# Another order of loads and units, and V of batch 0 sorted on TensorE, in a fused block-sorted attention and token-mixing kernel

## The chip, the cores and the metric

The kernel runs on one core of one Trainium2 chip. The metric is the time of one execution on the device in microseconds (us), the median over runs. A profile is of one execution; its times count from the first instruction.

## The reference, cut to what matters

The input has 4 batches of 8 heads, 768 rows of 64. The rows form 8 blocks of 96. K and V are mixed over blocks with an 8x8 matrix P for each head, which five rounds of row and column normalisation make out of sort_net. Attention works inside each block. Then a token mixer without softmax follows.

```
for _ in range(5):
    P = exp(P - max(P)); P = P / (sum_rows(P) + 1e-9); P = P / (sum_cols(P) + 1e-9)
k_sorted = einsum('bhij,bhjcd->bhicd', P, k_b)      # the same for v
x = softmax(scale * q_b @ k_sb.T) @ v_sb            # in each block of 96 rows
W = scale * (x @ w_q) @ (x @ w_k).T                 # 768 x 768 for each batch
out = relu(W @ x) @ w_out
```

## The kernel before, in words

**The order.** Nothing is scheduled by the compiler. A table of tokens, ORDER, is read from left to right, and each token calls one function u_*, which issues the instructions of one unit on the engines that the token names. Each engine keeps the order of its own instructions and waits for data and buffers by semaphores. A token is a kind, a batch, a number, and after colons an engine (A ScalarE, D VectorE, G GpSimd, S SyncE) or a PSUM bank, or both. A capital letter is work on TensorE into a bank, the small letter its eviction out of the bank:

- l: a load of one batch of q, k or v, or of weights (lp: w_q and w_k, lo: w_out). GpSimd issues it; it turns f32 in memory to bf16 (768 KB written). There are three buffers each for Qn, Kn and Vn, so batch 3 goes into batch 0's.
- a, c: the five normalisation rounds, on ScalarE and VectorE in turn. B spreads the result, and n makes the mixing matrices M of a batch (two buffers). Batch 0's M is made on VectorE out of PSUM, the others on GpSimd out of the copy PTR, in two instructions each.
- Z: fillers, products of zeros without use, so many as the number says.
- Q, q: turns Qn on TensorE (QT). K, k: sorts and turns Kn by a product with M (KT). In QT and KT the columns lie over the partitions.
- V, v: sorts Vn in three units, evicted to the one buffer Vs. Six SyncE DMAs (R, 132 KB each) regroup the rows of Vs into VT, in which the rows of a block lie over the partitions.
- S, e: scores and exponentials (E). P, r, x: product with VT (five units, the last a short one with 8 products in place of 14), reciprocal of the row sums, and scaling into X. One P unit needs all six R of its batch.
- T, t: turns X (XT). J, j: product with w_q and w_k (qkT). d: copies half of qkT to qD, on other partitions. W, w: turns qkT (wk). G, g: product of X and wk (Ab). H, h: product of Ab with qkT and qD, relu (mixT). O, o, s: product with w_out, eviction, output DMA.
- N: the gate. GpSimd copies one element of VT that all six R of a batch must have written; GpSimd's later loads stand behind it.

Y, y, F and f exist and are not in this order: they sort and turn V as K is sorted (into the KT buffer of the other batch), and turn it back in blocks of 96 rows into VT, without a DMA.

**Where the work waits.** GpSimd's queue holds the loads, M for batches 1 to 3 and four gates. SyncE's queue holds R, six of the eight qD copies and the output. A last part on GpSimd (guard) reads the reciprocals and decides whether a slow general path is run; it isn't. Line 147 is the matmul helper, 151 and 153 the copy helper on ScalarE and VectorE, so groups of the profile are told apart by tiles.

Of the kernel before, what the change touches and what calls it, by code (L numbers as in the profile page):

```python
# [16 lines left out]
ORDER = """
i02:D c00:D i00:G lq0 a01:A c01:D a02:A c02:D Z019:0 Q03:0 a03:A c03:D a04:A Q00:1 c04:D Q02:2 lq1
a05:A c05:D lv0 Z010:3 B00:3 lk0 n00:D:3 q00:A:1 n03:D:3 n02:D:3 Q13:1 i03:G Q11:4 q02:A:2 q03:D:0
Q12:2 q13:A:1 n01:D:3 Q01:5 Z011:6 V01:6 V00:0 q12:D:2 v00:A:0 u00:D:3 q01:D:5 V02:2 Q10:5 lk1  # L20
v02:A:2 Z09:0 K00:0 K01:2 n10:G q10:D:5 q11:A:4 K02:4 v01:A:6 K03:6 k00:A:0 lv1 k01:D:2 n11:G
k03:A:6 S00:0 k02:D:4 S01:2 S06:6 S04:4 e01:A:2 Z03:2 K10:2 e00:A:0 K13:0 e06:A:6 R01:S S02:6
k10:D:2 k13:D:0 K12:2 S05:0 e04:A:4 n21:G S03:4 R00:S R04:S e02:A:6 k12:D:2 lk2 e05:A:0 R03:S K11:6
lq2 e03:A:4 R02:S R05:S n20:G S14:2 e14:A:2 V12:0 k11:D:6 v12:D:0 V10:6 P03:4 r03:D:4 x03:D:4 V11:2
S11:0 v10:A:6 v11:A:2 P01:6 e11:A:0 P02:4 S12:2 S13:0 r01:D:6 x01:D:6 e12:A:2 r02:D:4 K22:6 k22:A:6
K20:2 e13:A:0 P04:6 x02:D:4 S15:4 e15:A:4 k20:D:2 P00:2 S10:0 r04:D:6 Q23:4 x04:D:6 R14:S r00:D:2
Q20:5 S16:6 e10:A:0 N05:G R15:S R10:S Q22:0 x00:D:2 Q21:3 q20:D:5 e16:A:6 K23:1 K21:5 T01:7 R11:S
q22:D:0 lv2 R12:S R13:S q23:A:4 k21:A:5 q21:D:3 lp k23:D:1 P12:3 t01:A:7 T02:0 r12:D:3 P11:5
x12:D:3 r11:D:5 V20:1 lq3 T03:7 t02:A:0 T00:0 V21:3 v20:A:1 x11:D:5 P13:1 t00:D:0 t03:A:7 P14:5
v21:A:3 r13:D:1 T11:7 J01:0 V22:3 x13:D:1 r14:D:5 j01:A:0 x14:D:5 P10:1 v22:A:3 r10:D:1 t11:D:7  # L30
n30:G x10:D:1 J00:0 S23:5 S20:3 T12:7 lk3 j00:A:0 e23:A:5 t12:D:7 e20:A:3 T13:0 W01:1 W00:2 n31:G
T10:5 S24:6 w01:D:1 t13:D:0 w00:D:2 S22:3 S25:0 t10:D:5 R23:S Q30:2 e24:A:6 Q31:5 Q33:6 N15:G G00:7
e22:A:3 q30:D:2 e25:A:0 Q32:2 d01:S K32:3 lv3 q31:D:5 q33:D:6 K31:5 K33:0 G01:7 q32:D:2 R20:S
k32:A:3 R24:S k31:A:5 k33:D:0 d00:S S21:2 J10:4 e21:A:2 g00:D:7 R25:S R21:S j10:D:4 S35:5 H02:0 lo
e35:A:5 R22:S H00:2 h00:A:2 J11:7 K30:4 j11:A:7 h02:D:0 k30:D:4 S32:0 W10:6 V30:2 w10:D:6 W11:7
V32:4 e32:A:0 P23:0 w11:A:7 v32:A:4 V31:6 v30:D:2 r23:D:0 v31:A:6 O04:2 x23:D:0 R31:S P20:3 S26:0
r20:D:3 R34:S S30:5 G10:7 G11:7 e26:A:0 S33:0 x20:D:3 H01:3 e30:A:5 o04:A:2 g10:D:7 P21:5 O05:2
h01:A:3 P22:3 d11:S r21:D:5 x21:D:5 T20:7 o05:A:2 e33:A:0 r22:D:3 t20:A:7 P24:5 R35:S x22:D:3
r24:D:5 O03:2 d10:S o03:A:2 O00:0 S36:3 H10:1 R32:S x24:D:5 S31:5 o00:A:0 R30:S e31:A:5 O02:7
h10:D:1 T22:0 e36:A:3 o02:A:7 t22:D:0 S34:5 s02:S H11:1 H12:3 R33:S T21:7 e34:A:5 N25:G O01:0  # L40
t21:A:7 P33:5 h11:D:1 T23:7 P30:1 h12:A:3 t23:A:7 o01:D:0 r33:D:5 P32:3 x33:D:5 s00:S r30:D:1 J20:0
O12:5 r32:D:3 s01:S P31:6 x30:D:1 j20:D:0 x32:D:3 O10:1 r31:D:6 O11:0 J21:4 j21:A:4 P34:2 x31:D:6
T32:6 o10:A:1 d21:S T31:7 r34:D:2 t31:A:7 T30:4 W20:1 N35:G x34:D:2 t30:A:4 T33:2 t32:D:6 t33:D:2
O15:3 J30:4 w20:D:1 W21:1 J31:2 j30:A:4 W30:4 j31:D:2 O14:7 W31:2 o11:A:0 w21:A:1 G20:1 o14:A:7
d30:D w30:A:4 s10:S d20:S G21:1 w31:D:2 G30:4 o15:A:3 G31:4 g20:A:1 o12:A:5 H20:6 h20:A:6 H22:2
H21:0 d31:D g30:D:4 h22:D:2 O13:4 O21:7 o13:A:4 s11:S h21:D:0 O20:6 o20:A:6 H30:2 s12:S H31:4
h31:A:4 o21:D:7 O24:7 O25:6 O22:4 h30:D:2 O23:5 O31:3 o25:A:6 o23:A:5 o24:D:7 s20:S o22:D:4 H32:0
O30:4 s22:S o31:D:3 O33:3 s21:S h32:D:0 o33:D:3 o30:A:4 O35:0 O34:1 o34:A:1 s31:S O32:3 s30:S
o35:D:0 o32:A:3 s33:S s35:S s34:S s32:S
"""  # L50


# [1 line left out]
def kernel(  # L54
# [91 lines left out]
    def mm(o, w, x, start=True, stop=True, t=False):  # L146
        nc.tensor.matmul(o, w, x, is_transpose=t, start=start, stop=stop, skip_group_check=True)  # L147

    def copy(e, o, i):
        if e == "A":  # L150
            nc.scalar.copy(o, i)  # L151
        else:
            nc.vector.tensor_copy(o, i)  # L153
# [7 lines left out]

    def u_a(b, n, e, bank):
        nc.scalar.activation(Pv, Pv, ACT.Exp)
        if n == 2:
            for j in range(NB):
                mm(PS[:, 7, 0:SP], idb, idb[:, j * SP:(j + 1) * SP], start=(j == 0), stop=(j == NB - 1))
            nc.scalar.copy(m_p, PS[:, 7, 0:SP])
        elif n == 3:
            nc.scalar.copy(Lx.rearrange("p a j s -> p (a j) s"),
                           idb[0:BH, 0:BH].unsqueeze(2).to_broadcast([BH, BH, SP]))  # L170

    def u_c(b, n, e, bank):
        if n == 0:
# [46 lines left out]
                                in_=src[b, h0:h1].rearrange("h (p r) d -> p h (r d)", p=P))  # L220

    def u_B(b, n, bank):

# [78 lines left out]
        ENG[e].dma_start(out=VT[b % 2].rearrange("(s r) i h x -> r s i (h x)", r=R6)[n],  # L302
                         in_=Vs[0][:, n].rearrange("p h e -> p (h e)"))

    def u_N(b, n, e, bank):

        nc.gpsimd.tensor_copy(gate[0:R6, :], VT[b % 2][0:R6, NB - 1, H - 1, 0:1])  # L307
# [338 lines left out]
```

## Time and profile before

| | us |
|---|---|
| median of 3 runs | 111.21 (110.87 to 113.28) |
| span of the profiled execution | 109.3 |
| TensorE busy | 94.8 (87%), of it fillers 14.4 |
| VectorE, ScalarE, GpSimd busy | 71.1, 67.6, 26.8 |

The file gives no separate time for the profiled execution; its span is 109.3 us, 1.9 below the median of the runs, and what lies around the span is counted as these 1.9 us. In the strips of the profile a digit is a tenth of busy time in a fortieth of the span. In a group or row, the tile written stands left of the arrow and the tiles read right of it; "x" counts instructions; in square brackets stands how long the engine was idle before, and what ended that.

### The profile page before, as it was taken

Reading aid. Unit: us, or ns where it says so; the run is one execution under the profiler, and the core shown is the slowest. Engines: PE = TensorE matmul, PEld = TensorE weight load, DVE = VectorE, ACT = ScalarE, POOL = GpSimd, SP = SyncE. Lnnn points to the kernel's source line nnn. Section 1 sums busy time; section 2 is a strip of 40 time slices with the busy share of each in tenths; the row PEclk is TensorE's granted clock in tenths of the full one; section 3 lists DMA queues with packets and bytes.
Section 4 is the critical chain, followed back from the end, with each engine's and each line's share of the span. In section 5 each row is a group of like instructions: output and inputs, shape, how many; then the busy total and the mean of one; then the engine's idle time right before and its main releaser. Section 6 shows DMA issues by size and latency. Waiting matters only on the chain.

```text
span 109.3 us, 3462 instructions
## 1 busy us (share of the span) xinstructions
PE 94.8 (87%) x1460; PEld 64.3 (59%) x1460; DVE 71.1 (65%) x140; ACT 67.6 (62%) x96; POOL 26.8 (24%) x46
## 2 busy tenths in 40 slices
PE   4997999986978759999959999999999993999950
PEld 2335557463767648897948687746858672443410
DVE  2676681060959984799956898778898431974720
ACT  4224314897589874698976998899706671463240
POOL 7960029069079700330000000000004700000000
PEclk9999999999599995999999999999999999999999
DMA  0899999999999999999999914670360050097872
GB/s 3 91 201 204 203 204 206 203 235 248 229 210 199 218 254 239 188 209 202 218 242 248 201 25 117 164 244 6 127 261 17 6 218 4 40 418 309 352 307 112
DMA packets 20225, 20.16 MB, mean 185 GB/s; under 512 B 2032, under 2 KB 18288, under 8 KB 20208
## 3 DMA queue, kind: packets, MB, share of 16 engines
q0 software_dynamic: 14064, 10.09, 61.1%
q1 hardware_dynamic: 6144, 9.84, 26.7%
q8 instruction: 11, 0.18, 0.6%
q14 instruction: 6, 0.05, 0.1%
HBM read 20.19 MB, written 6.29 MB: 242 GB/s over the span
## 4 chain that ended last, share of the span: by engine, by line
PE 53%; DMA 34%; POOL 5%; issue 2%; DVE 2%; ACT 1%; POOLq 0%; ACTq 0%; DVEq 0%
PE ps L147 53%; DMA Kn<-in_k_dram 15%; DMA Qn<-in_q_dram 14%; DMA qD<-qkT 4%; POOL Qn L219 2%; POOL M L240 1%; DVE QT L153 1%; DVE KT L153 1%; POOL Kn L219 1%; POOL Vn L219 1%; ACT ot L151 1%; POOL idb L191 0%; POOL idb L190 0%; POOLq L191 0%; DVE qkT L153 0%
## 5 line engine op out<-in xcount | busy, mean ns | idle before, releaser
L321 ACT ACTIVATE E<-ps 96x960 bf16<-96x960 f32 (+1 forms) x28 | 24.1, 898 | 5.2 <-PE ps L147 5.1
L147 PE MATMUL ps<-wo,mixT 128*128 128x512 bf16 x96 | 22.7, 379 | 0.0
L350 DVE TENSOR_TENSOR X<-ps,Rall 96x896 bf16<-96x896 f32 (+1 forms) x20 | 20.1, 1005 | 0.6
L151 ACT COPY ot<-ps 128x512 f32<-128x512 f32 x17 | 10.0, 588 | 8.7 <-PE ps L147 8.0
L147 PE MATMUL ps<-fil 128*128 128x512 bf16 x52 | 14.4, 433 | 0.4 <-ACT Vs L151 0.2
L153 DVE CAST KT<-ps 128x768 bf16<-128x768 f32 x10 | 9.4, 956 | 7.7 <-PE ps L147 7.5
L147 PEld LDWEIGHTS <-mixT 128*128 128x128 bf16 x96 | 8.6, 98 | 9.4 <-issue 0.6
L151 ACT CAST Vs<-ps 128x1024 bf16<-128x1024 f32 x10 | 9.9, 1019 | 4.2 <-PE ps L147 4.0
L147 PE MATMUL ps<-VT,E 96*128 96x65 bf16 x256 | 10.9, 193 | 1.0 <-DVE X L350 0.3
L147 PEld LDWEIGHTS <-E 96*128 96x128 bf16 x256 | 9.8, 97 | 2.8 <-issue 1.3
L147 PE MATMUL ps<-idb,Qn 128*64 128x128 bf16 x192 | 8.1, 244 | 3.3 <-DMA Qn<-in_q_dram 1.9
L240 POOL TENSOR_TENSOR M<-PTR,m_p 128x512 bf16<-128x512 bf16 x6 | 7.9, 1323 | 12.1 <-DVE PTR L153 8.4
L412 DVE TENSOR_SCALAR mixT<-ps 128x1024 bf16<-128x1024 f32 x7 | 8.5, 1222 | 3.0 <-PE ps L147 3.0
L147 PE MATMUL ps<-QT,KT 64*128 64x96 bf16 x256 | 10.0, 213 | 0.4 <-DVE KT L153 0.2
L153 DVE COPY QT<-ps 128x768 bf16<-128x768 bf16 x11 | 5.9, 553 | 6.7 <-PE ps L147 6.7
L307 POOL COPY gate<-VT 6x1 bf16<-6x1 bf16 x4 | 0.7, 177 | 38.3 <-DMA VT<-Vs 38.3
L147 PEld LDWEIGHTS <-fil 128*128 128x128 bf16 x52 | 5.4, 109 | 7.4 <-issue 3.4
L147 PEld LDWEIGHTS <-Qn 128*64 128x64 bf16 x192 | 6.7, 124 | 4.6 <-DMA Qn<-in_q_dram 2.7
L147 PE MATMUL ps<-M,Kn 128*64 128x128 bf16 x192 | 8.0, 238 | 1.6 <-DMA Kn<-in_k_dram 1.3
L147 PEld LDWEIGHTS <-KT 64*128 64x128 bf16 x256 | 6.9, 99 | 3.5 <-issue 1.9
L147 PEld LDWEIGHTS <-Kn 128*64 128x64 bf16 x192 | 6.7, 121 | 3.5 <-DMA Kn<-in_k_dram 2.2
L147 PE MATMUL ps<-idb,X 96*128 96x96 bf16 x128 | 7.5, 206 | 0.0
(74 smaller groups left out, 129.0 us busy)
## 6 DMA issues: line engine op xcount, KB each, us to landing
out_dram<-ot SPq DMA_DIRECT2D x9, 512.0 KB, 3.3
VT<-Vs SPq DMA_DIRECT2D x24, 132.0 KB, 6.4
Qn<-in_q_dram POOLq DMA_DIRECT2D x4, 768.0 KB, 12.8
Vn<-in_v_dram POOLq DMA_DIRECT2D x4, 768.0 KB, 14.9
Kn<-in_k_dram POOLq DMA_DIRECT2D x4, 768.0 KB, 18.1
out_dram<-ot SPq DMA_DIRECT2D x6, 256.0 KB, 2.0
wo<-in_moe_w_out_dram POOLq DMA_DIRECT2D x1, 512.0 KB, 17.4
qD<-qkT SPq DMA_DIRECT2D x6, 48.0 KB, 3.3
```

The costliest lines, as they stand in the source:

```text
L147: nc.tensor.matmul(o, w, x, is_transpose=t, start=start, stop=stop, skip_group_check=True)
L151: nc.scalar.copy(o, i)
L153: nc.vector.tensor_copy(o, i)
L219: nc.gpsimd.dma_start(out=t[b % NIN][:, h0:h1].rearrange("p h r d -> p h (r d)"), in_=src[b, h0:h1].rearrange("h (p r) d -> p h (r d)", p=P))
L240: ENG[e].tensor_tensor(out=M[b % 2][:, h0:h0 + hn], in0=src.unsqueeze(2).to_broadcast([P, hn, SP, NB]), in1=m_p.unsqueeze(1).unsqueeze(3). ...
L307: nc.gpsimd.tensor_copy(gate[0:R6, :], VT[b % 2][0:R6, NB - 1, H - 1, 0:1])
L321: nc.scalar.activation(E[b % 2][:, n, 0:2 * w * BLK].rearrange("p (t a c) -> p a t c", a=2, c=BLK), PS[0:BLK, bank:bank + 2, 0:w * BLK].re ...
L350: nc.vector.tensor_mul(xo.rearrange("p (a t d) -> p a t d", a=2, d=D), avps(bank, w)[:, :, :, 0:D], Rall[:, b, n, :, 0:w].unsqueeze(3).to_ ...
L412: nc.vector.tensor_relu(o, i)
```

## The change

The whole table ORDER is written anew. The rest of the edit is what the new table needs:

- GpSimd's queue starts with the loads of q and k of batch 0, ahead of the identity and the memsets. The loads' order was q0, q1, v0, k0, k1, v1, k2, q2, v2, w_q, w_k, q3, k3, v3, w_out; now it is q0, k0, q1, v0, v1, k1, w_q, w_k, k2, q2, w_out, v2, q3, k3, v3.
- The four gates are gone, with the buffer gate.
- V of batch 0 goes through four Y and four F units with their evictions, in place of three V and six R.
- Five of the eight qD copies run on GpSimd and three on VectorE; none is a DMA.
- Fillers are 22 in three places (52 in five before). The spreading of small constants is a unit of its own (B01, p). All other units stand in a new order, with engines and banks newly given.
- u_D, a transposing DMA, is defined and not used.

```diff
-i02:D c00:D i00:G lq0 a01:A c01:D a02:A c02:D Z019:0 Q03:0 a03:A c03:D a04:A Q00:1 c04:D Q02:2 lq1
...
+i02:D Z03:0 lq0 c00:D lk0 a01:A c01:D i00:G i03:G B01:0 p01:A a02:A p00:A:0 c02:D lq1 lv0 a03:A c03:D lv1
...
-    gate = sb.tile([P, 1], BF16, name="gate")
...
-        if n == 2:
-            for j in range(NB):
-                mm(PS[:, 7, 0:SP], idb, idb[:, j * SP:(j + 1) * SP], start=(j == 0), stop=(j == NB - 1))
-            nc.scalar.copy(m_p, PS[:, 7, 0:SP])
...
+    def u_p(b, n, e, bank):
+        if n == 0:
+            copy(e, m_p, PS[:, bank, 0:SP])
...
-    def u_N(b, n, e, bank):
-
-        nc.gpsimd.tensor_copy(gate[0:R6, :], VT[b % 2][0:R6, NB - 1, H - 1, 0:1])
...
     def u_d(b, n, e, bank):
         o, i = (t[b % 2][p:p + DH, n * 384:(n + 1) * 384] for t, p in ((qD, DH), (qkT, 0)))
-        if e == "S":
-            nc.sync.dma_start(out=o, in_=i)
+        if e == "G":
+            nc.gpsimd.tensor_copy(o, i)
         else:
             copy(e, o, i)
```

What the table does shows in the engines' queues. In the rows that follow, a name's suffix is a buffer: M_107 and M_108 are the two buffers of M (batches 0 and 2, 1 and 3), Kn_74 is batch 2's, Qn_69 and Kn_72 those of batches 0 and 3. DMASW0 to DMASW7 are the eight semaphores on which GpSimd's loads tell of their landing, taken in turn.

GpSimd before, from the second K load to the load of q of batch 3:

```order
L219 DMA Kn_73<-in_k_dram 128x8x384
L240 TENSOR_TENSOR M_108<-PTR,m_p 128x512 [waits DVE_49,Activation_49]
L219 DMA Vn_76<-in_v_dram 128x8x384
L240 TENSOR_TENSOR M_108<-PTR,m_p 128x512
L240 TENSOR_TENSOR M_107<-PTR,m_p 128x512 [waits PE_49]
L219 DMA Kn_74<-in_k_dram 128x8x384
L219 DMA Qn_71<-in_q_dram 128x8x384
L240 TENSOR_TENSOR M_107<-PTR,m_p 128x512
L307 COPY gate<-VT_85 6x1 [waits DMAHW4_49,DMAHW5_49,DMAHW3_49,DMAHW6_49,DMAHW2_49,DMAHW1_49]
L219 DMA Vn_77<-in_v_dram 128x8x384 [waits DMASW0_49]
```

GpSimd now, from the load of K of batch 2, the ninth DMA on this queue:

```order
L215 DMA Kn_74<-in_k_dram 128x8x384 [waits DMASW0_49]
L215 DMA Qn_71<-in_q_dram 128x8x384 [waits DMASW1_49]
L210 DMA wo<-in_moe_w_out_dram 128x4x512 [waits DMASW2_49]
L215 DMA Vn_77<-in_v_dram 128x8x384 [waits DMASW3_49]
L215 DMA Qn_69<-in_q_dram 128x8x384 [waits DMASW4_49,PE_49]
L239 TENSOR_TENSOR M_108<-PTR,m_p 128x512 [waits Activation_49]
L239 TENSOR_TENSOR M_108<-PTR,m_p 128x512
L215 DMA Kn_72<-in_k_dram 128x8x384 [waits DMASW5_49,PE_49]
```

M of batch 1 (M_108) stood between the first six loads; now it stands behind the load of q of batch 3, which waits for the landing of v of batch 1 (DMASW4).

ScalarE now, from the first of batch 1's three evictions of sorted V (Vs) to the last eviction ahead of the first P unit of that batch:

```order
L147 COPY Vs_84<-ps 128x8x2x64 [waits PE_49]
L147 COPY KT_83<-ps 128x768 [waits PE_49]
L147 COPY KT_83<-ps 128x768 [waits PE_49,Activation_49]
L315 ACTIVATE E_88<-ps 96x2x2x96 [waits PE_49]
L147 COPY Vs_84<-ps 128x8x2x64 [waits DVE_49,PE_49]
L147 COPY Vs_84<-ps 128x8x2x64 [waits PE_49]
L315 ACTIVATE E_88<-ps 96x2x5x96 [waits DVE_49,PE_49]
L315 ACTIVATE E_88<-ps 96x2x5x96 [waits PE_49]
L315 ACTIVATE E_88<-ps 96x2x5x96 [waits DVE_49,PE_49]
L147 COPY KT_82<-ps 128x768 [waits PE_49]
L315 ACTIVATE E_88<-ps 96x2x5x96 [waits PE_49]
L147 COPY XT_91<-ps 128x768 [waits DVE_49,PE_49]
```

Behind these come one more E and two QT evictions, then the first P unit's banks are free. Before, ScalarE had two of batch 1's three Vs evictions one behind the other:

```order
L321 ACTIVATE E_88<-ps 96x2x5x96
L151 COPY Vs_84<-ps 128x8x2x64 x2
L321 ACTIVATE E_88<-ps 96x2x5x96 x2
L151 COPY KT_82<-ps 128x768
L321 ACTIVATE E_88<-ps 96x2x5x96 x3
L321 ACTIVATE E_88<-ps 96x2x2x96
L151 COPY QT_80<-ps 128x768
```

The first of the three moved ahead of two KT evictions of the same batch; the other two stand behind them and a short E.

More of the change, by code (lines that the diff above doesn't have):

```diff
@@ L17 @@
 ORDER = """
-i02:D c00:D i00:G lq0 a01:A c01:D a02:A c02:D Z019:0 Q03:0 a03:A c03:D a04:A Q00:1 c04:D Q02:2 lq1
[L19 to L47, printed above, removed]
@@ L48 @@
-O30:4 s22:S o31:D:3 O33:3 s21:S h32:D:0 o33:D:3 o30:A:4 O35:0 O34:1 o34:A:1 s31:S O32:3 s30:S
-o35:D:0 o32:A:3 s33:S s35:S s34:S s32:S
+i02:D Z03:0 lq0 c00:D lk0 a01:A c01:D i00:G i03:G B01:0 p01:A a02:A p00:A:0 c02:D lq1 lv0 a03:A c03:D lv1
+Z010:0 lk1 a04:A c04:D lp a05:A c05:D lk2 Q03:0 lq2 Q02:1 q03:A:0 Q01:2 B00:3 lo q01:D:2 q02:A:1 Q00:0 n03:D:3
+lv2 n01:D:3 K03:1 n02:D:3 K01:4 q00:D:0 k03:A:1 lq3 K02:6 n00:D:3 k01:A:4 k02:D:6 S05:0 u00:A:3 S02:4 e05:A:0
+S03:6 n10:G S04:2 e02:A:4 Q13:0 Q11:1 n11:G q13:D:0 e03:A:6 K00:4 q11:D:1 Q10:0 k00:A:4 S06:6 lk3 Q12:1
@@ new lines @@
+e06:A:6 S00:4 q12:D:1 q10:A:0 S01:6 e01:A:6 Y03:0 y03:A:0 e04:A:2 Y01:6 Y00:0 y01:D:6 y00:A:0 n20:G F03:3
+Z09:2 f03:A:3 e00:A:4 F01:0 F00:1 f01:D:0 V12:2 f00:D:1 Y02:4 v12:A:2 P04:6 n21:G P01:0 r04:D:6 y02:A:4
+x04:D:6 P00:2 R15:S r01:D:0 R14:S lv3 K13:4 r00:D:2 x01:D:0 K11:6 k13:A:4 k11:D:6 K10:0 S16:4 x00:D:2 e16:A:4
+V11:6 V10:4 v11:A:6 k10:D:0 T00:3 n30:G F02:2 v10:A:4 t00:D:3 R13:S S11:0 f02:D:2 K12:6 R12:S e11:A:0 S10:4
+n31:G k12:D:6 R10:S P02:2 e10:A:4 P03:0 R11:S r02:D:2 x02:D:2 S13:6 K20:4 e13:A:6 r03:D:0 T01:2 x03:D:0
@@ new lines @@
+k20:A:4 S14:6 t01:D:2 e14:A:6 T03:0 K22:3 t03:A:0 K23:1 k22:D:3 S15:6 T02:5 e15:A:6 k23:D:1 Q23:4 Q20:3
+q23:A:4 Q22:6 t02:D:5 q20:D:3 q22:A:6 S12:0 P13:6 e12:A:0 J00:5 r13:D:6 x13:D:6 P10:3 j00:A:5 S24:0 d00:G
+W00:5 r10:D:3 e24:A:0 P14:6 x10:D:3 J01:2 S20:0 j01:D:2 S25:3 e20:A:0 r14:D:6 w00:D:5 d01:G W01:2 x14:D:6
+Q21:5 e25:A:3 P11:0 q21:D:5 S26:6 w01:D:2 T13:5 r11:D:0 e26:A:6 x11:D:0 V22:2 t13:A:5 V21:6 v22:A:2 P12:4
+v21:D:6 V20:0 T10:2 R24:S r12:D:4 G00:3 v20:D:0 t10:A:2 R23:S K21:6 R22:S G01:3 k21:A:6 x12:D:4 R21:S Q31:0
@@ new lines @@
+g00:A:3 Q33:1 R20:S q31:D:0 H00:2 S21:4 R25:S q33:D:1 H02:6 h00:A:2 T11:0 h02:D:6 e21:A:4 T12:1 S22:2 t12:D:1
+H01:6 t11:A:0 S23:4 h01:D:6 O00:1 e22:A:2 J11:0 o00:A:1 e23:A:4 K32:6 j11:D:0 K31:1 k32:D:6 d11:G J10:3
+k31:D:1 K33:4 j10:A:3 K30:6 W10:3 d10:D k30:A:6 O02:0 k33:D:4 w10:A:3 W11:7 o02:A:0 S36:5 S35:3 w11:D:7 S32:1
+e36:A:5 G10:7 e35:A:3 P22:5 e32:A:1 G11:7 r22:D:5 x22:D:5 V32:3 P23:0 v32:A:3 O05:2 g10:D:7 r23:D:0 x23:D:0
+R35:S H11:6 o05:A:2 H10:4 R34:S Q30:3 h11:A:6 h10:D:4 T22:0 V30:1 q30:A:3 P24:6 t22:D:0 O11:5 v30:A:1 r24:D:6
@@ new lines @@
+x24:D:6 S30:3 o11:D:5 Q32:0 R31:S e30:A:3 P21:6 R30:S P20:1 q32:A:0 r21:D:6 V31:3 x21:D:6 T23:5 v31:A:3 O03:0
+r20:D:1 t23:D:5 x20:D:1 S34:6 R32:S o03:A:0 S33:4 T21:3 R33:S e33:A:4 O04:0 t21:D:3 s01:S e34:A:6 S31:1
+o04:D:0 H12:3 T20:5 e31:A:1 h12:D:3 O10:6 s02:S P32:0 o10:D:6 P33:2 r32:D:0 O01:4 s10:S r33:D:2 x32:D:0 O15:6
+x33:D:2 P34:0 o15:A:6 O14:7 t20:D:5 P31:2 o01:D:4 o14:A:7 J20:5 r31:D:2 s00:S r34:D:0 x34:D:0 J21:4 s12:S
+j20:A:5 x31:D:2 T32:7 d20:G j21:A:4 W20:0 T33:1 d21:G W21:6 w20:D:0 T31:2 t33:D:1 w21:A:6 G20:0 t31:D:2 P30:5
@@ L50 @@
+t32:D:7 G21:0 r30:D:5 x30:D:5 O12:7 g20:A:0 H21:0 o12:A:7 H20:2 H22:4 h21:D:0 h20:A:2 T30:6 O13:7 t30:D:6
+O22:3 h22:D:4 o13:A:7 J30:2 s11:S o22:A:3 J31:7 j30:D:2 O21:6 d30:D j31:A:7 d31:D W30:7 W31:5 o21:A:6 O23:4
+w31:D:5 w30:A:7 G30:7 o23:A:4 O24:6 s21:S G31:7 o24:A:6 O20:4 g30:A:7 H32:6 o20:D:4 H31:1 h32:A:6 O25:5
+h31:D:1 s20:S H30:3 o25:A:5 O35:7 h30:D:3 s22:S O34:6 o35:D:7 O31:5 o34:A:6 s35:S O32:7 s34:S o31:A:5 O30:6
+s31:S o32:A:7 O33:5 s32:S o30:A:6 s30:S o33:A:5 s33:S
 """
@@ L163, in u_a @@
         nc.scalar.activation(Pv, Pv, ACT.Exp)
-        if n == 2:
-            for j in range(NB):
-                mm(PS[:, 7, 0:SP], idb, idb[:, j * SP:(j + 1) * SP], start=(j == 0), stop=(j == NB - 1))
-            nc.scalar.copy(m_p, PS[:, 7, 0:SP])
-        elif n == 3:
-            nc.scalar.copy(Lx.rearrange("p a j s -> p (a j) s"),
-                           idb[0:BH, 0:BH].unsqueeze(2).to_broadcast([BH, BH, SP]))
+    def u_p(b, n, e, bank):
+        if n == 0:
+            copy(e, m_p, PS[:, bank, 0:SP])
+        else:
+            copy(e, Lx.rearrange("p a j s -> p (a j) s"),
+                 idb[0:BH, 0:BH].unsqueeze(2).to_broadcast([BH, BH, SP]))
     def u_c(b, n, e, bank):
@@ L222, in u_B @@
     def u_B(b, n, bank):
+        if n == 1:
+            for j in range(NB):
+                mm(PS[:, bank, 0:SP], idb, idb[:, j * SP:(j + 1) * SP], start=(j == 0), stop=(j == NB - 1))
+            return
         for i in range(NB):
@@ L360, in u_t, with u_D @@
         copy(e, XT[b % 2][:, n, :], bf(bank)[:, 0:S])
+    def u_D(b, n, e, bank):
+        ENG[e].dma_start_transpose(out=XT[b % 2][:, n, :].rearrange("p (i c) -> p i c", i=NB),
+                                   in_=X[b % 2][:, n].rearrange("p i m -> p (i m)"))
     def u_J(b, n, bank):
@@ L609 @@
         b, n = int(name[1]), int(name[2:])
-        if kind.isupper() and kind not in "RN":
+        if kind.isupper() and kind not in "RD":
             fns[kind](b, n, int(arg[0]))
```

## The prediction

> **What bounds the kernel now.** I read the page first: its strips by time, then the chain that ended last.
>
> ```profile
> PE   4997999986978759999959999999999993999950
> PEclk9999999999599995999999999999999999999999
> DMA  0899999999999999999999914670360050097872
> ...
> PE 53%; DMA 34%; POOL 5%; issue 2%; DVE 2%; ACT 1%; POOLq 0%; ACTq 0%; DVEq 0%
> ```
>
> The kernel has two halves. Up to its slice 23 (a slice is 2.73 us) the DMA engines are full with loads. TensorE is full from about slice 17 to the end. The chain says the same: 53% TensorE, 34% loads. So the first half ends with a wait for data and the second with TensorE itself. The stretches give sums (columns: length, busy time with count for TensorE matmul, weight load, VectorE, ScalarE, GpSimd, then granted clock, DMA share, GB/s).
>
> ```profile
> 8.90:21.10 12.20, 11.66 (x158) 7.21 (x158) 6.08 (x20) 5.76 (x8) 3.50 (x3) 1.00 1.32 204
> 45.20:105.40 60.20, 57.05 (x856) 38.69 (x856) 43.83 (x72) 40.73 (x60) 5.45 (x12) 1.00 0.68 175
> 105.40:109.30 3.90, 0.00 (x0) 0.00 (x0) 0.00 (x0) 0.59 (x1) 0.00 (x0) 0.93 0.50 190
> ```
>
> In the last 60.2 us before TensorE's end it works 57.05 us. The rest is a wait for qD and one 1.28 us stop. The timeline of TensorE has the border at 45.22: the first P unit of batch 1, which needs all six VT transfers of that batch. GpSimd's gate, which waits for the same six, runs in the same moment.
>
> ```profile
> 8.98 1.20 PE L147 MATMUL ps<-idb,Qn 128*64 128x128 bf16 x36 [0.78 <-DMA Qn<-in_q_dram]
> ...
> 45.22 0.60 PE L147 MATMUL ps<-VT,E 96*128 96x65 bf16 x14 [0.25 <-DVE KT L153]
> ...
> 57.39 0.49 PE L147 MATMUL ps<-idb,Qn 128*64 128x128 bf16 x11 [1.28 <-issue]
> ...
> 92.09 0.28 PE L147 MATMUL ps<-qD,Ab 64*128 64x256 bf16 x1 [1.74 <-DMA qD<-qkT]
> ```
>
> ```profile
> 1.48 2.03 POOL L219 DMA_DIRECT2D Qn<-in_q_dram  x2 [0.17 <-issue]
> ...
> 34.13 1.35 POOL L240 TENSOR_TENSOR M<-PTR,m_p 128x512 bf16<-128x512 bf16 x1
> 35.38 0.94 POOL L219 DMA_DIRECT2D Kn<-in_k_dram  x1
> ...
> 45.22 0.18 POOL L307 COPY gate<-VT 6x1 bf16<-6x1 bf16 x1 [7.55 <-DMA VT<-Vs]
> ```
>
> The two orders are alike in one thing that makes the sum short. Counted in the tables, what follows the first P unit of batch 1 (P12 before, P13 in the changed kernel) is the same work: 15 P, 14 S, 8 J, 8 W, 8 G, 12 H, 24 O, 6 V. The changed kernel has one Q and one K more and three T fewer, which cancel. So the question is when that unit starts, and how much TensorE idles behind it.
>
> **The change, part by part.** *Loads start earlier.* The first load now stands ahead of the identity, whose first instruction ran at 0.74 and pushed the load to 1.48: 0.74 us gained. q0 lands at 8.98 - 0.74 = 8.2. A load writes 768 KB; at 204 GB/s that is 3.85 us. In the new order: k0 12.1, q1 15.9, v0 19.8, v1 23.6, k1 27.5.
>
> *No gates.* By themselves they are worth nothing: the DMA strip is full while they wait, since earlier loads are still queued. What hides their removal is that queue. Without it a gate would cost the time it waits, 7.55 us in the row above.
>
> *The ninth load waits instead.* The order of GpSimd's queue shows eight landing semaphores, so each load from the ninth on waits for the landing of the one eight before it. q3's load waits for v1 (23.6), and both M instructions of batch 1 stand behind it: 23.6 + 0.94 (issue, as of k3) + 2 x 1.35 (M) = 27.2. Before, M of batch 1 was made while nothing waited for it. Now V12, the first V of batch 1, waits. TensorE alone would be there at about 24.5: v0 lands at 19.8, and three Y, three F and nine fillers fill 4.7 us behind it (1.1 + 1.5 + 2.1, by the rows that follow).
>
> *V of batch 0 on TensorE.* Four Y and four F units replace three V, and six VT transfers go. Prices are from these groups and rows (group columns: busy and mean ns; row columns: start, length).
>
> ```profile
> 16.67 1.50 PE L147 MATMUL ps<-Vn,M 128*128 128x128 bf16 x24
> ...
> 18.82 2.10 PE L147 MATMUL ps<-fil 128*128 128x512 bf16 x9 [0.20 <-ACT Vs L151]
> 21.13 1.53 PE L147 MATMUL ps<-M,Kn 128*64 128x128 bf16 x48 [0.20 <-DMA Kn<-in_k_dram]
> ```
>
> ```profile
> L321 ACT ACTIVATE E<-ps 96x960 bf16<-96x960 f32 x24 | 22.6, 967 | 2.8 <-PE ps L147 2.7
> L350 DVE TENSOR_TENSOR X<-ps,Rall 96x896 bf16<-96x896 f32 x16 | 17.4, 1085 | 0.4
> L151 ACT CAST Vs<-ps 128x1024 bf16<-128x1024 f32 x10 | 9.9, 1019 | 4.2 <-PE ps L147 4.0
> L153 DVE CAST KT<-ps 128x768 bf16<-128x768 f32 x10 | 9.4, 956 | 7.7 <-PE ps L147 7.5
> L151 ACT COPY XT<-ps 128x768 bf16<-128x768 bf16 x8 | 6.3, 806 | 0.1
> L151 ACT CAST KT<-ps 128x768 bf16<-128x768 f32 x6 | 4.7, 800 | 3.2 <-PE ps L147 3.2
> L151 ACT COPY QT<-ps 128x768 bf16<-128x768 bf16 x5 | 3.9, 791 | 1.8 <-PE ps L147 1.8
> L345 DVE RECIPROCAL Rall<-ps 96x14 f32<-96x14 f32 x16 | 3.6, 230 | 1.9 <-PE ps L147 1.8
> L350 DVE TENSOR_TENSOR X<-ps,Rall 96x512 bf16<-96x512 f32 x4 | 2.7, 686 | 0.1
> ```
>
> Y is sorted like K: 1.53 us for four. F is eight turns, at V's 0.50 a unit 2.0. Minus V's 1.50 that is 2.0 us more on TensorE. It lies ahead of V12, under the wait for M; without that cover it would cost its 2.0. The evictions of F have no row; between XT's 0.81 and Vs' 1.02 on ScalarE I take 1.0, since its 1024 elements are Vs' number. They too fall ahead of V12.
>
> *From V12 to the first P of batch 1.* V12 (0.50), Y02 (0.38) and P04 end at about 28.4. VectorE then owes P04, P01 and P00 two short and three long instructions that K10's banks wait for (0.20 + 0.69 + 0.23 + 0.23 + 1.09 = 2.44), then k11 (0.96), whose banks V11 needs: 31.8. V11 0.5 makes 32.3. ScalarE has v11 and v10 (2 x 1.02), five E (4.84), one KT (0.80), one XT (0.81) and two QT (1.58) in its order until the banks of P13 are free: 10.07, so 42.4. The other condition is VT. The issues of batch 1's six transfers, and the times to landing of all 24:
>
> ```profile
> 33.60 3.78 SPq L302 DMA_DIRECT2D VT<-Vs  x6
> ```
>
> ```profile
> DMA to landing us min/median/max: 2.3/6.4/8.2
> ```
>
> v10 ends at 34.3, two issues of 0.6 (3.78 for six) follow, the last at about 35.3. Landing is then between +6.4 and +8.2: 41.7 to 43.5. The 11.6 us from first issue (33.60) to gate (45.22) agree from the other side: the first issue, behind v12 at about 28.8, gives 40.4. I take 42.8, nearer the later end because a last transfer queues behind five. The lead over 45.22 is 2.4 us.
>
> *qD by engines.* Six DMAs become five GpSimd copies and one more on VectorE. A GpSimd copy of 384 elements lies between the gate's 0.18 (1 element) and M's 1.35 (512, two inputs); I take 0.6. For batches 0 and 1 the H units stand far behind, for batch 2 the two W and two G units lie between: hidden even at 1.35. The VectorE copies of batch 3 follow their qkT. The 1.74 us wait at 92.09 goes; next to be late there is the eviction of qkT.
>
> *Fillers and output.* 52 become 22; the 30 removed stood before slice 10, in front of waits. The output's end is alike: 3.90 us behind TensorE's last matmul.
>
> *The sum.* 42.8 + 57.0 (the same work) + 1.3 (the stop of 57.39 stays) + 1.2 = 102.3. The 1.2 is an estimate for thinner cover: VectorE has 48.4 us of the order's evictions behind P13, at the groups' means, against 46.3 before behind P12; the 2.1 more may show from nothing to 2.1. With 3.90 the span is 106.2, against 109.3. The median of the runs, 111.21, is 1.9 over that profiled span; so 108.1.
>
> **The clock of TensorE.** The same view of stretches shows what idling costs.
>
> ```profile
> 23.40:26.80 3.40, 1.94 (x36) 1.02 (x33) 0.53 (x1) 3.17 (x5) 3.39 (x4) 1.00 1.22 251
> 26.80:30.20 3.40, 3.39 (x68) 2.77 (x64) 2.78 (x3) 1.62 (x2) 0.35 (x1) 0.51 1.27 231
> ...
> 54.10:57.50 3.40, 2.12 (x69) 1.83 (x64) 1.98 (x5) 2.65 (x3) 0.00 (x0) 1.00 1.23 243
> ```
>
> Behind a stretch with 1.94 of 3.40 us busy the clock was 0.51; behind one with 2.12 the strip at the top stays at 9. A halved stretch holds 1.7 us less work. The wait for M (24.5 to 27.2) would make such a stretch.
> The Trainium skill, "TensorE: Matmul & The Clock Gate", Part 1, gives the half rate after at least one idle window of about 3.4 us; by that rule nothing here idles long enough, the clock stays and the sum is 108.1. The trace disagrees: 1.94 us of work in the window did not keep it.
>
> **Rivals.** *Full gain.* VT lands at 41.0, P13 follows, no new small waits: 41.0 + 57.0 + 1.3 + 3.9 + 1.9 = 105.1. For it: 40.4 from the first issue. Against: ScalarE's 10.07 us, which alone give 42.4.
> *The lead is eaten.* A halved clock behind the wait for M (1.7) and the late M push P13 to 44.5, and another 0.8 is lost behind: 44.5 + 57.0 + 1.3 + 2.0 + 3.9 + 1.9 = 110.6. For it: the rows of the clock, fewer fillers. Against: the stretch 27 to 31 is VectorE's, so part of the loss is covered.
> *Slower: loads crowd out VT.* With up to eight loads queued at once, each of the six VT transfers takes 1 us longer than in the 11.6 us from 33.60 to 45.22. Six more us: P13 at 48.8, 114.1. It decides against the change once VT lands later than 48.1 (108.1 + 5.3 = 113.4). Against: three loads were queued there before, and the DMA share was full.
> *The gates did nothing,* and the change is only its order: that is in the forecast already.
>
> **How the numbers follow.** Forecast 0.50 (107 to 109.5), full gain 0.13, eaten 0.25, slower 0.12. About 2% is what a measurement of this kernel can tell from no change: 109.0 and 113.4 are the borders. Of the forecast's case some nine in ten lie under 109.0: 0.45 + 0.13 = 0.58 faster; 0.05 + 0.25 = 0.30 the same; 0.12 slower. The range reaches from the full gain's 105.1 to 111.6, an eaten lead with one more us; it leaves out the slower case and a tail.
>
> **What would show it.** First Q matmul at about 8.2 (right) or 9; M of batch 1 not before v1 has landed, at 25 to 27, and TensorE idle before the V units of batch 1; first P of batch 1 at 42.8, over 45 would be the eaten lead; granted clock under 1 behind 27; no wait for qD; busy TensorE of 57 us behind P13, with idle of 2.5. A P13 later than 48, or idle of over 6 us behind it, would make the prediction wrong.

## The result and the profile after

The changed kernel takes 109.44 us (median; 109.27 to 109.55). The ratio to the kernel before is 0.9854 (95% interval 0.9818 to 0.9891), so it is 1.5% faster, about half of the 2.8% that was forecast. That ratio is taken from the two shorter executions of the kernel before (110.87 and 111.21 us); the other two took 113.28 and 113.36, and against the median of all four (112.25) the changed kernel is 2.5% faster. In the executions of this study the kernel before ran at 110.9 to 114.2 us, far more widely than the changed one; the last section says what a trace shows of that. Variants are therefore compared by their own times and profiles, and a ratio is always to the kernel before on the same chip.

The strips of the changed kernel's page, for TensorE, its granted clock and DMA:

```profile
span 107.4 us, 3466 instructions
...
PE   5399477559889979599998999999999999999950
...
PEclk9999999985999999999999999999999999999999
DMA  0999999999999999999999400323974503145982
```

The two halves are still there: loads fill the DMA engines up to slice 22, TensorE is full from slice 18 on. One dip of the clock is left where there were two, and it lies earlier. The changed kernel's chain of work, here in order of time (start, length, what), now runs through the steps that the prediction had named:

```profile
6.68 18.09 DMA Vn<-in_v_dram
24.82 0.49 issue
25.31 0.88 POOL Qn L215
26.20 2.58 POOL M L239 x2
28.83 1.22 PE ps L143 x24
...
36.75 7.55 DMA VT<-Vs
44.44 0.61 PE ps L143 x14
```

v of batch 1 lands at 24.8. The load of q of batch 3, which waits for that landing, is issued. M of batch 1 is made, and V12 goes on at 28.83. The last VT transfer leaves at 36.75, and the first P of batch 1 starts at 44.44. The same places in TensorE's timeline of the changed kernel:

```profile
20.91 0.86 PE L143 MATMUL ps<-M,Vn 128*64 128x128 bf16 x24 [1.18 <-DMA Vn<-in_v_dram]
...
24.21 3.21 PE L143 MATMUL ps<-fil 128*128 128x512 bf16 x8 [0.22 <-issue]
...
28.15 0.39 PE L143 MATMUL ps<-Vn,M 128*128 128x128 bf16 x4
28.83 0.40 PE L143 MATMUL ps<-Vn,M 128*128 128x128 bf16 x4 [0.30 <-POOL M L239]
...
44.44 0.59 PE L143 MATMUL ps<-VT,E 96*128 96x65 bf16 x14 [1.23 <-DMA VT<-Vs]
```

V12 needs M in two halves: its first four products start at 28.15, the other four at 28.83, when the second half of M is there. The first P came 0.78 us earlier than before (45.22), not 2.4. Stretches of the changed kernel, the last of them behind the first P:

```profile
20.00:23.40 3.40, 1.60 (x40) 1.44 (x41) 0.96 (x1) 2.75 (x4) 0.89 (x1) 1.00 1.31 205
23.40:26.90 3.50, 3.28 (x15) 1.58 (x14) 0.00 (x0) 2.30 (x3) 1.57 (x2) 0.51 1.32 204
...
44.40:103.50 59.10, 57.98 (x846) 37.97 (x856) 45.18 (x73) 39.04 (x59) 5.75 (x12) 1.00 0.63 168
```

From the first P to TensorE's end it is 59.0 us, where it was 60.1; the wait for qD is gone. So the span fell by 0.8 in front of the first P and 1.1 behind it.

### The profile page after: what moved, and what is told of

It reads as the page before. It is cut to its first block, busy times and chain, and to the rows that moved or that the text cites. A ratio compares the mean times of both kernels' runs of the same rounds, so it can differ in the third digit from the quotient of the medians.

```text
span 107.4 us, 3466 instructions
## 1 busy us (share of the span) xinstructions
PE 91.2 (85%) x1475; PEld 61.4 (57%) x1486; DVE 72.3 (67%) x143; ACT 68.8 (64%) x99; POOL 28.4 (26%) x47
## 4 chain that ended last, share of the span: by engine, by line
PE 43%; DMA 24%; DVE 15%; POOL 8%; issue 4%; ACT 3%; DVEq 0%; SPq 0%; POOLq 0%; ACTq 0%
PE ps L143 43%; DMA Vn<-in_v_dram 17%; DMA VT<-Vs 7%; DVE X L344 6%; POOL M L239 2%; DVE mixT L410 2%; POOL Qn L215 2%; DVE Rall L339 1%; DVE Vs L149 1%; ACT Vs L147 1%; ACT E L315 1%; DVE ot L149 1%; POOL Kn L215 1%; DVE KT L149 1%; POOL Vn L215 1%
## 5 line engine op out<-in xcount | busy, mean ns | idle before, releaser
L344 DVE TENSOR_TENSOR X<-ps,Rall 96x896 bf16<-96x896 f32 (+1 forms) x20 | 19.8, 1000 | 0.4
L371 POOL COPY qD<-qkT 64x384 bf16<-64x384 bf16 x5 | 2.5, 503 | 43.9 <-ACT qkT L147 31.2
L143 PE MATMUL ps<-fil 128*128 128x512 bf16 x21 | 9.1, 607 | 2.0 <-DVE fil L191 1.2
L143 PEld LDWEIGHTS <-KT 64*128 64x128 bf16 (+1 forms) x288 | 8.5, 98 | 4.1 <-issue 1.9
L147 ACT CAST KT<-ps 128x768 bf16<-128x768 f32 x10 | 7.9, 798 | 3.8 <-PE ps L143 3.7
L410 DVE TENSOR_SCALAR mixT<-ps 128x1024 bf16<-128x1024 f32 x8 | 9.8, 1222 | 0.5 <-PE ps L143 0.4
L147 ACT CAST Vs<-ps 128x1024 bf16<-128x1024 f32 x7 | 7.0, 1019 | 4.3 <-PE ps L143 3.8
L143 PE MATMUL ps<-QT,KT 64*128 64x96 bf16 x256 | 9.1, 204 | 0.5 <-ACT KT L147 0.5
L143 PE MATMUL ps<-M,Kn 128*64 128x128 bf16 x192 | 7.2, 221 | 0.8 <-DVE X L344 0.4
L143 PEld LDWEIGHTS <-X 96*128 96x128 bf16 x128 | 6.2, 98 | 2.2 <-issue 0.6
L339 DVE RECIPROCAL Rall<-ps 96x14 f32<-96x14 f32 (+1 forms) x20 | 4.3, 223 | 4.7 <-PE ps L143 4.6
```

Source lines behind the costliest of these rows:

```text
L339: nc.vector.reciprocal(Rall[:, b, n, :, 0:w], avps(bank, w)[:, :, :, D])
L344: nc.vector.tensor_mul(xo.rearrange("p (a t d) -> p a t d", a=2, d=D), avps(bank, w)[:, :, :, 0:D], Rall[:, b, n, :, 0:w].unsqueeze(3).to_ ...
L371: nc.gpsimd.tensor_copy(o, i)
L410: nc.vector.tensor_relu(o, i)
```

## The experiments

### M of batch 1 ahead of the loads

Three kernels: in the first, two loads change places with M in GpSimd's queue; the second only drops the nine fillers; the third does both.

```diff
-... n03:D:3 lv2 n01:D:3 ... k01:A:4 lq3 ...
-... n11:G q13:D:0 ...
+... n03:D:3 n01:D:3 ... k01:A:4 ...
+... n11:G lv2 lq3 q13:D:0 ...
```

```diff
-... F03:3 Z09:2 f03:A:3 ...
+... F03:3 f03:A:3 ...
```

> The changed kernel with the loads of v of batch 2 and q of batch 3 moved behind M of batch 1 in GpSimd's queue. Theory A (M of batch 1, held by the landing that the q3 load waits for, delays the first P of batch 1): M is ready by 21 us instead of 28.8, V12 starts when v1 has landed (24.8) and the first P of batch 1 moves from 44.4 to about 42.4, where ScalarE's chain ends; time 107.4. Theory B (the nine fillers of Z09, at half clock, keep TensorE busy until 27.3 and the F units until 28.2 anyway): V12 moves by 0.3 to 0.7 us only; time 108.9.

> The changed kernel without the nine fillers in front of the second F unit. Theory A: nothing, since M of batch 1 still holds V12 at 28.8; time 109.4, or up to 1 us more if a clock halved for longer meets the work behind V12. Theory B alone would have V12 3 us earlier, but with M not ready it can't be: both theories expect 109.4 here, and the run tells what the fillers do for the clock (granted clock of the 3.4 us behind 26.9: 1.00 with them).

> Both edits. Theory A: the same as M early alone, 107.4. Theory B: only now V12 comes to 25 to 26 us; first P of batch 1 at about 42.4, time 107.4, where M early alone gave 108.9. A third outcome, 109 or more: the first P of batch 1 is held by ScalarE's evictions or a halved clock, and neither M nor the fillers are its price.

Measured, in this order: 108.47 us (107.69 to 109.29; ratio 0.9733, interval 0.9529 to 0.9937), 111.17 us (0.9918, 0.9857 to 0.9979), 107.48 us (107.21 to 108.79; 0.9659, 0.9467 to 0.9851). In the kernel with M early, GpSimd and TensorE show:

```profile
17.36 2.58 POOL L240 TENSOR_TENSOR M<-PTR,m_p 128x512 bf16<-128x512 bf16 x2
```

```profile
23.59 2.11 PE L144 MATMUL ps<-fil 128*128 128x512 bf16 x9
26.43 0.61 PE L144 MATMUL ps<-Vn,M 128*128 128x128 bf16 x8
...
42.73 0.59 PE L144 MATMUL ps<-VT,E 96*128 96x65 bf16 x14 [1.41 <-ACT E L316]
```

```profile
23.40:26.80 3.40, 3.40 (x39) 2.37 (x37) 0.55 (x1) 2.26 (x3) 0.88 (x1) 1.00 1.32 203
```

M is ready by 20 instead of 28.8, and the first P starts at 42.73, which is the 42.8 of the prediction. The 1.7 us show in full in the profiled execution (span 105.8 against 107.4). But two things differ between these two profiles, M and the clock. In the changed kernel's profile the clock was halved under the fillers, which took 3.21 us instead of 2.11, and TensorE reached V12 only at 28.15; M held it 0.7 us more, to 28.83. With M early the clock stayed full there (the stretch above), and V12 started at 26.43. So of the 2.4 us that V12 moved between these two executions, 1.7 go with the clock and 0.7 with M.

Both limits have to go. The executions with M early at 107.7 and 107.8 us had a mean clock of 1.00, as theory A has it; those at 109.1 and 109.3 had 0.984 and 0.975, which is near theory B's 108.9, though no profile of them shows where they lost it. With M late a fuller clock gained nothing: the kernel with the identity first, below, took 109.51 at a mean clock of 0.996 and 109.61 at 0.979.

Without the fillers, the place of M shows by itself. With M early, V12 starts at 25.5 and the first P at 42.40:

```profile
42.40 0.59 PE L144 MATMUL ps<-VT,E 96*128 96x65 bf16 x14 [1.23 <-DMA VT<-Vs]
```

With M late, TensorE idles, and two windows of the clock are halved. The stretches of that kernel, and its timeline:

```profile
23.90:27.50 3.60, 1.06 (x17) 0.90 (x15) 1.28 (x2) 1.92 (x3) 1.77 (x2) 1.00 1.35 201
27.60:31.00 3.40, 2.38 (x29) 1.76 (x30) 0.00 (x0) 1.13 (x2) 3.04 (x4) 0.50 1.53 195
31.00:34.30 3.30, 3.30 (x61) 3.15 (x61) 2.36 (x6) 1.30 (x2) 2.92 (x3) 0.50 1.31 203
```

```profile
27.97 0.61 PE L144 MATMUL ps<-Vn,M 128*128 128x128 bf16 x4 [2.93 <-POOL M L240]
...
46.40 0.59 PE L144 MATMUL ps<-VT,E 96*128 96x65 bf16 x14 [1.20 <-DMA VT<-Vs]
```

The wait for M is open there with 2.93 us, and the first P comes 4.0 us later than with M early. It comes 2.0 us later than in the changed kernel: 0.4 is M's own (29.2 against 28.8), the rest goes with the two halved windows. The expectation had allowed the clock 1 us at most. So the fillers are not mere ballast while M is late.

### M of batch 1 later still

```diff
-... n10:G Q13:0 Q11:1 n11:G q13:D:0 ... lk3 Q12:1 ...
+... Q13:0 Q11:1 q13:D:0 ... lk3 n10:G n11:G Q12:1 ...
```

> The changed kernel with M of batch 1 one load later still in GpSimd's queue, behind the load of k of batch 3, which waits for k1 (28.5). Theory A (what stands between M and the first P of batch 1 is a fixed 15.6 us, so M's delay goes straight into the time): M ready at about 32.6 instead of 28.8, first P of batch 1 at 48.2, time 113.2, and up to 1.7 us more if the longer wait halves the clock. Rival (other waits cover M): less than half of the 3.8 us shows, time under 111.3.

It took 115.03 us (ratio 1.022, interval 1.0118 to 1.0322). TensorE's timeline of this kernel:

```profile
31.50 0.40 PE L144 MATMUL ps<-Vn,M 128*128 128x128 bf16 x4 [4.68 <-POOL M L240]
32.75 0.61 PE L144 MATMUL ps<-Vn,M 128*128 128x128 bf16 x4 [0.86 <-POOL M L240]
...
50.08 0.59 PE L144 MATMUL ps<-VT,E 96*128 96x65 bf16 x14 [1.35 <-DMA VT<-Vs]
```

V12 goes on at 32.75, 3.9 later than in the changed kernel, and the first P 5.6 later, at 50.08. The 1.7 beyond the delay are what the expectation gave for a halved clock, and the stretch 32.1 to 38.8 of this kernel has a granted clock of 0.50. With the runs above this shows that M's place in GpSimd's queue sets the first P of batch 1 wherever M comes later than TensorE's own way to V12. The time between the two is not fixed, though: 15.6 us in the changed kernel, 17.3 here.

### The first load behind the identity again

```diff
-i02:D Z03:0 lq0 c00:D lk0 a01:A c01:D i00:G i03:G ...
+i02:D Z03:0 i00:G lq0 c00:D lk0 a01:A c01:D i03:G ...
```

> The changed kernel with the identity made ahead of the first two loads on GpSimd, as before. Step of the prediction (the load ahead of the identity gains 0.74 us): q of batch 0 lands 0.74 us later than in the changed kernel, first P of batch 1 and the time 0.7 us later, 110.1. What the changed kernel's profile suggests instead (first load issued at 1.27 against 1.48, landed at 9.00 against 8.93): q lands within 0.2 us of 9.0, time 109.3 to 109.7.

It took 109.60 us (109.51 to 109.71; ratio 0.9721, 0.963 to 0.9811). Loads' issues in this kernel, then in the changed one:

```profile
1.02 0.29 POOL L188 TENSOR_SCALAR_AFFINE_SELECT idb<-idb 128x128 bf16<-128x128 bf16 x1
1.46 1.13 POOL L216 DMA_DIRECT2D Qn<-in_q_dram  x1
```

```profile
1.27 1.13 POOL L215 DMA_DIRECT2D Qn<-in_q_dram  x1 [0.82 <-POOLq L629]
```

The load's issue begins at 1.27 instead of 1.46, not at 0.74: with nothing ahead of it, GpSimd is still idle for 0.82. q lands at 9.05 against 9.00; in the other kernels with the load first it lands at 8.64 to 8.97. So the load's new place is worth 0.4 us at most, and v of batch 1 shows none of it (25.0 here, 24.8 to 25.2 in the others). The step of the prediction that counted 0.74 us here is refuted.

### qD, from both sides

In the kernel before, the six DMAs become copies on VectorE; in the changed one, they become DMAs again.

```diff
 the kernel before:
-... d01:S ... d00:S ... d11:S ... d10:S ... d21:S ... d20:S ...
+... d01:D ... d00:D ... d11:D ... d10:D ... d21:D ... d20:D ...
 the changed kernel:
-... d00:G ... d01:G ... d11:G ... d10:D ... d20:G ... d21:G ...
+... d00:S ... d01:S ... d11:S ... d10:S ... d20:S ... d21:S ...
+        elif e == "S":
+            nc.sync.dma_start(out=o, in_=i)
```

> The kernel before with its six qD DMAs made copies on VectorE (0.25 us each), nothing else. Theory A: the 1.74 us wait for qD at 90.3 goes and nothing takes its place: 1.7 us less than the kernel before, about 109.3, so that this part alone is worth as much as the whole change. Rival: the six copies (1.5 us of VectorE) delay evictions that TensorE waits for, or the eviction of qkT is late next: 0.5 us less or nothing.

> The changed kernel with the six qD copies of batches 0 to 2 made SyncE's DMAs again, as in the kernel before. Theory A (the wait for qD was a place of its own, and all that the change gained behind the first P of batch 1): a wait of 1 to 2.5 us of TensorE ahead of an H unit comes back, span 108.5 to 110, time 110.4 to 111.9, so about the kernel before. Rival (in this order the H units stand far enough behind): under 0.5 us, time 109.4 to 109.9.

The kernel before with copies took 109.47 us (109.41 to 110.55; ratio 0.983, 0.966 to 1.0), as fast as the whole change. The interval reaches 1.0, so the profile has to decide. Its stretch behind the first P:

```profile
45.20:103.80 58.60, 56.93 (x856) 38.64 (x856) 45.51 (x79) 40.85 (x60) 5.45 (x12) 1.00 0.68 175
```

58.60 us instead of 60.20 with the same work: the 1.74 us wait is gone, and the 1.7 us of VectorE more are hidden. But the changed kernel with DMAs took 109.83 us (109.73 to 110.14; ratio 0.9669, 0.9619 to 0.9719), only 0.4 more than with copies. Its view of the tile qD lists what the engines that write or read qD waited for:

```profile
its engine sat idle before it (us, times) until:
  ACT qkT L148: 0.3, 1
```

In the kernel before, the same view has 1.7 us until the DMA of qD; here no product stands idle for a DMA of qD, and TensorE's timeline has no wait of over 0.3 us behind the first P. So theory A falls for this kernel and its rival holds: in the new order the H units stand far enough behind. Either the copies or the new order removes the wait, and the change has both.

### The gates

```diff
-... N05:G ... N15:G ... N25:G ... N35:G ...
```

> The kernel before without its four gates, nothing else. Theory A (a gate never empties the queue of loads, so it neither costs nor saves): VT of batch 1 lands at 45.0 within 1 us, the load of v of batch 2 at 45.9 within 1 us, time as before within 0.7 us. Rival (gates keep loads from crowding out VT): VT of batch 1 lands 1 to 3 us later and the time is 1 to 3 us longer. Rival the other way (gates hold loads back): loads end 1 to 3 us earlier, and the time is shorter by up to that.

It took 112.96 us (111.19 to 113.89), with the kernel before at 113.23 to 114.19 beside it (ratio 0.9829, 0.9749 to 0.991). With runs of one kernel 2.7 us apart, this ratio does not settle a question of 0.7 us. The place does. GpSimd's timeline has the load of v of batch 2 issued at 27.28 instead of 30.82, and TensorE's has the first P where it was (45.22 with gates):

```profile
27.28 0.94 POOL L216 DMA_DIRECT2D Vn<-in_v_dram  x1
```

```profile
45.44 0.61 PE L144 MATMUL ps<-VT,E 96*128 96x65 bf16 x14 [1.79 <-DMA VT<-Vs]
```

The load is issued 3.5 us earlier and lands at 45.89 instead of 45.85; the last of the six VT transfers lands at 45.05 instead of 44.98. Neither rival shows at this place: the gate did not hold the load back, and did not protect VT.

### V of batch 0 through DMA in the new order

```diff
-... Y03:0 y03:A:0 ... Y01:6 Y00:0 y01:D:6 y00:A:0 ... Y02:4 ... F02:2 ...
+... V01:0 v01:A:0 R02:S R03:S ... V00:6 V02:0 v00:D:6 R00:S R01:S v02:A:0 R04:S R05:S ...
-... P04:6 ... P01:0 ... (r, x of these, P00, T00)
+... the same units ahead of P02:2 ...
```

> The changed kernel with V of batch 0 as before: three V units and six transfers in place of four Y and four F; the first three P units of batch 0 and their followers moved behind the S units of batch 1, where they can wait. Theory A (the new order of loads needs the sorting on TensorE, since v0 lands only at 20.9 here): VT of batch 0 lands at about 33, the transfers of batch 1 queue behind them, and the first P of batch 1 starts at 46 to 48 instead of 44.4; time 111 to 113. Rival (the transfers are hidden, and four Y, four F and their evictions are work too much): first P of batch 1 at 44 or earlier, time 109.4 or less.

It took 119.33 us (ratio 1.0491, 1.0437 to 1.0546). The direction is theory A's; the size isn't. VT of batch 0 lands at 33.5 and VT of batch 1 at 47.0, as theory A has it, but the first P came only at 55.33, released by ScalarE's eviction of QT. This kernel's stretches show why its span of 118 us is no price of the transfers alone:

```profile
27.00:29.50 2.50, 0.67 (x8) 0.45 (x8) 0.00 (x0) 0.00 (x0) 2.17 (x2) 1.00 1.49 237
29.60:53.40 23.80, 17.09 (x259) 14.49 (x260) 11.76 (x18) 10.12 (x12) 6.96 (x6) 0.50 1.28 222
```

With work missing here and there, TensorE's clock stays halved for 24 us. So putting the transfers back into this order costs 10 us, and 8.3 us of the first P's delay lie behind the landing of VT; that V of batch 0 has to be sorted on TensorE is not shown, since a well-made order with six transfers more was not tried.

### Towards a faster version

One kernel has M early and spreads fillers over three waits. A second one, besides, puts the three V units of batch 1 together, to send VT earlier.

```diff
 first:
+... Z05:3 B00:3 ... Z05:0 Y03:0 ...
-... F03:3 Z09:2 ...
+... F03:3 Z04:2 ...
 second, in addition:
-... V12:2 Y02:4 v12:A:2 ... V11:6 V10:4 v11:A:6 ... v10:A:4 ...
+... V12:2 V11:6 v12:A:2 V10:4 ... v11:D:6 ... v10:A:4 ... Y02:4 ...
```

> M of batch 1 early, and the fillers put where TensorE waits: five ahead of the spreading of P, five ahead of the first Y unit, four in place of nine ahead of the second F unit. Theory A (with M early what is left to lose is the clock, whose halving moves from run to run): granted clock 0.98 to 1.00 in every run, first P of batch 1 at 42.0 to 42.7, times between 106.9 and 107.8 where M early gave 107.7 to 109.3. Rival (fillers delay the work behind them more than the clock saves): 108 or more.

> M of batch 1 early and the fillers put where TensorE waits, and besides the three V units of batch 1 one behind the other, with evictions on ScalarE, VectorE, ScalarE, ahead of the last Y unit, the P units of batch 0 and the K units of batch 1. Theory A (with M early VT's transfers are still what the first P of batch 1 waits for): the last of the six is issued at 29.5 to 30.5 instead of 34.3, VT of batch 1 lands at 37.5 to 38.5, and the first P starts when ScalarE's evictions let it, at 41.0 to 41.8 instead of 42.4; time 106.0 to 107.0. Rival (the transfers now run ahead of k and q of batch 2 and hold those up): Q of batch 2 no earlier than 41.5, first P at 42.4 or later, time 107.2 or more.

The first took 108.09 us (107.20 to 108.81; ratio 0.9533, 0.9464 to 0.9603): first P at 42.39 as expected, but its runs still spread by 1.6 us, with granted clocks of 0.984 to 0.998. The fillers did not make the clock safe, and it is no better than M early without the nine fillers (107.48). The second took 109.02 us (107.68 to 109.23; ratio 0.9635, 0.9507 to 0.9762), and theory A falls. Its timeline:

```profile
44.08 0.59 PE L144 MATMUL ps<-VT,E 96*128 96x65 bf16 x14 [0.60 <-ACT QT L148]
```

The last transfer is issued at 30.5 instead of 34.3 and VT lands at 38.9, 3.4 us earlier; yet the first P starts 1.7 us later, released by ScalarE's eviction of QT. With M early the transfers are no longer what alone holds it. The rival's numbers are met (Q of batch 2 at 41.97), but not its reason: q of batch 2 lands at 40.1 instead of 39.8. In TensorE's timeline the last Y unit, now behind the three V units and a wait of 1.12 us for their eviction, starts at 28.13 instead of 26.00, and the P units of batch 0 at 28.59 instead of 26.46. A halved window (33.0 to 36.4) lies behind; how much of the 1.7 us is whose was not taken apart.

## Why the prediction was half right

| step | forecast | measured |
|---|---|---|
| q0 lands | 8.2 | 9.00 |
| v1 lands | 23.6 | 24.8 |
| M of batch 1 ready | 27.2 | 28.8 |
| first P of batch 1 | 42.8 | 44.44 |
| from there to TensorE's end | 59.5 | 59.0 |
| behind it, to the span's end | 3.9 | 4.0 |
| span | 106.2 | 107.4 |

The mechanism was right: the work behind the first P is the same in both kernels, the ninth load's wait holds M, M holds V12, and V12 the first P. From M to the first P it was 15.6 us, in the sum and in the profile. The step that failed is a term's size: M of batch 1, and with it V12, at 27.2. It came at 28.8, and the first P at 44.44 instead of 42.8. The start of the loads is 0.8 of these 1.6 us: 0.74 was taken off, and the load's new place gained nearly nothing. The loads q1, v0 and v1 together took 0.4 more than three times 3.85, and from the landing to the next issue passed 0.5 us, which the sum had left out; the issue and M were 0.2 shorter than taken.

The step beside it failed too: "TensorE alone would be there at about 24.5". TensorE was there at 28.15. v of batch 0 landed at 20.9 instead of 19.8, two waits for evictions (0.56 and 0.34) were not counted, and the halved clock, which the prediction saw only behind the wait for M, fell on the fillers (3.21 us instead of 2.1). In this execution M at 27.2 would have moved V12 by 0.7 us at most. With M early and the clock full, the first P came at 42.73; with M late, at 50.08.

The sum put 2.4 us of the gain in front of the first P and 0.7 behind it; measured were 0.8 and 1.1. That the stretch behind it came so near the forecast is in part luck, as two errors cancel. Small waits were taken as 2.5 and came to 1.1: the stop of 1.28 us shrank to 0.29, and the 1.2 for thinner cover did not show. The work measured 58.0 instead of 57.0. Right as well: no gates, nothing in the timeline; the wait for qD gone; GpSimd's qD copy at 0.50 to 0.51, taken as 0.6. But the wait's end was put down to the copies alone, and the DMAs in the new order do not wait either. And the kernel before with copies alone is as fast as the whole change.

The clock's part went as the rows said: 1.60 of 3.40 us busy, and 0.51 in the next window. The Trainium skill's rule in "TensorE: Matmul & The Clock Gate", Part 1, half rate after an idle window, would have had no dip there. The trace disagrees: windows with 1.06 to 1.94 us of work were followed by a halved one. The rival in which a halved clock eats the lead had the first P at 44.5, and it came at 44.44. So that rival was half true: the halved window lay at 24 us instead of behind 27, in front of M's arrival, and the further 0.8 us behind the first P were not lost.

## What to carry to other kernels

In this kernel a load that reuses a landing semaphore stops everything behind it in its queue until the earlier load has landed (M by 8.8 us here); put what later work needs ahead of it, and see in the queue's order which landing each load waits for. When two schedules have the same work behind one unit, the difference lies in that unit's start plus the idle time behind it, and both can be read from one row each. When two things arrive within a microsecond of each other, here M and TensorE's own work, moving one of them gains little until the other moves too. Before a filler is taken out, look at how full its window of the clock stays.

## What the runs showed of the hardware

TensorE's clock is granted in windows of 3.41 us: every halved stretch while TensorE works lasts that long in the traces or a whole multiple of it (6.83 us with M late, 23.9 with V of batch 0 through DMA). The grid of the windows lies differently in each execution: the halved window begins at 23.46 in the changed kernel and at 22.29 in the one with qD's DMAs, which has the same work up to there. A window with little work is often followed by a halved one: 1.06 and 1.60 us busy were followed by 0.50 and 0.51 in the stretches above, and 2.12 in the prediction's by the full clock. But no border of busy time follows. With M late, 1.61 us between 25.2 and 28.6 were followed by the full clock, and only the window behind that, nearly empty, by 0.50:

```profile
28.60:32.00 3.40, 0.40 (x4) 0.23 (x4) 0.00 (x0) 0.00 (x0) 2.75 (x3) 1.00 1.34 203
```

Where the grid cuts a gap in two, neither window may be empty enough, so the same gap can cost nothing more in one execution and up to 1.7 us in another. The wait for qD shows it. In the kernel before (first stretch) it is 1.74 us long and the grid cuts it at 91.7, and the clock stays full. In the kernel without gates (the other two stretches) it is 1.76 us long and lies in one window:

```profile
88.30:91.70 3.40, 2.06 (x33) 1.63 (x33) 0.96 (x3) 1.93 (x5) 0.00 (x0) 1.00 0.37 129
```

```profile
91.00:94.40 3.40, 1.59 (x18) 0.82 (x16) 0.92 (x2) 1.09 (x2) 0.00 (x0) 1.00 0.02 4
94.40:97.80 3.40, 3.40 (x9) 1.19 (x9) 2.43 (x3) 0.82 (x2) 0.00 (x0) 0.50 0.27 112
```

Both of these executions have two halved windows and a mean clock of 0.97, but spans of 109.3 and 112.1 us. In the first the halved windows begin at 26.8 and 40.5, ahead of the first P, which had to wait for VT until 45 anyway; in the second at 46.6 and 94.4, where the end of the kernel waits for TensorE, and its work behind the first P takes 59.67 us instead of 57.05. So the place of a halved window tells its price, and the mean clock does not. That the wide spread of the kernel before comes from this is likely, not shown, as only one of its executions left a profile. With qD copied, so without the gap, it took 109.41 to 110.55; the changed kernel, with no gap of over 0.3 us behind the first P, stays within 0.3 us in its four.
